# An attention and gated-MLP block in fp32 on one core: GpSimd's work pinned to program order, the fifth block's weights and the second pair's k strips loaded at other times, the last two heads' query blocks in another order, and loads of finished heads two ahead

## The chip, the core and the metric

The kernel runs on one core of one Trainium2 chip. The metric is the device time of one execution in microseconds (us); before the change it is 2733.96 us, the median of 3 runs (2732.69 to 2734.78). The engines are TensorE (PE, matmuls and transposes), VectorE (DVE), ScalarE (ACT), GpSimd (POOL) and SyncE (SP), each with its own instruction stream; SP issues most DMA transfers, POOL the rest.

## The reference

The input x is 2048 rows of D = 576. It is normalised, and goes through 32 heads of attention with 18 features each and through an MLP of width F = 4608 with a relu gate; the result is x plus attention times the silu of the MLP.

```python
xn = _layernorm(x, axis=-1)
s = _A_ref(xn, A_wqkv, A_wo)      # 32 heads, softmax(q k^T / sqrt(18)) v, then @ wo
g = _silu(_B_ref(xn, W_gate, W_up, W_down))   # h = relu(x W_gate) * (x W_up); h @ W_down
return x + s * g
```

## The kernel before

**Precision.** An fp32 product is made of three: each operand is split into a rounded part (hi) and the rest (lo), and hi x hi, hi x lo and lo x hi are added up (`PRODUCTS`, L97). Weights are split on POOL (`split_pool`, L93 to L95: a cast and a subtraction), results in PSUM on ACT and DVE (`split_full`, L89 to L91).

**Stage 1, up to 225 us.** Row groups of 512 (g = 0 to 3) are normalised, transposed and multiplied by the q, k and v weights. A group has four blocks of q and k columns (b = 0 to 3, `qk_block`), a fifth of 64 columns for two groups at once (`qk_last`, weights wqk4), and v (`v_block`). The results go from tiles of a ring of four ("hh": hh for q and k, ev for v) to DRAM (qd, kd, vd) by transfers that POOL issues (L300, L332). `weights` (L194) loads raw weights into a ring of two (rgw) by SP and splits them on POOL; `spill` (L282) writes a group's transposed rows to DRAM by SP.

**Stage 2, 225 to 2563 us.** 144 units, k = 36 x g + n. A unit takes 128 of the 4608 columns for one row group: `up(k)` multiplies by the gate and up weights (PE tile pg, weights gw, loaded and split one unit ahead by `up_weights(k + 1)`, ring of two), `up_end` makes h and its split hh (ACT hi, POOL lo, L461), and after every second unit `down` multiplies two units by the down weights dw into py and adds to y. Between the matmuls of a unit stand steps of attention of a pair of heads u = 0 to 15: `max_steps` (pm: row maxima of the scores of pair u + 1) and `exp_steps` (psx: scores of pair u, exponential p on ACT), then `attend` (po: p times va, the values with a column of ones). The first nine units hold only `max_steps` of pair 0, nine units go with each later pair. In units k < 9 ACT copies py and POOL adds it. `max_rows` (L543) writes the maxima of two query blocks (512 queries each) as extra rows into their qT tiles, by eight transfers of 2 KB on SP (L560), so that psx gives scores less the maximum. `load_q` and `load_k` load q and k strips from DRAM. `gate_steps` (L501) makes the silu of finished rows: exp on ACT, +1 and six reciprocals on DVE, a product on POOL, and a store to gd.

**Stage 3, 2563 us to the end.** Only the scores of the last pair (u = 15) are left, block by block (`exp_steps` with last=True), and between them runs the generator `outputs`: down(143), then for each tile k of 128 rows `heads(k)` (load 512 finished features o4 from od, transpose, split into hf), `rows_of` (gate row gt, input row xr), the product with wo (pw: `first4`, plus `last1` for the last 64 features, which come from o5 by `o5_rows`), gate, add, store. Tiles of query block 3 come first with their first 512 features alone, and are finished last.

**Order.** Instructions given to `tc.keep_in_program_order` keep their place behind the one traced before on their engine; for the others a scheduler chooses the order on their engine. PE's matmuls and transposes are all kept. PSUM has a ring of five banks for pm, psx and small transposes (`shared`), one for po, and a ring of two for pg, py, tps and pw (`bank`).

Of the kernel before, what the change touches and what calls it, by code (L numbers as in the profile page):

```python
# [19 lines left out]
def kernel(  # L20
# [68 lines left out]
    def split_full(dhi, dlo, ps):  # L89
        nc.scalar.activation(dhi, ps, AF.Copy)  # L90
        nc.vector.tensor_tensor(dlo, ps, dhi.bitcast(F32), ALU.subtract)  # L91

    def split_pool(hi, lo, raw):  # L93
        nc.gpsimd.tensor_copy(hi, raw)  # L94
        nc.gpsimd.tensor_tensor(lo, raw, hi.bitcast(F32), ALU.subtract)  # L95

# [65 lines left out]
    def max_steps(u, h):  # L162

        rows = slice(h * R, h * R + KA)
        for g in range(NQ):
            if h == 0:
                load_q(*((u, g + 1) if g + 1 < NQ else (u + 1, 0)))
                if g % 2 == 0:
                    mxs[u, g // 2] = at.tile([P, 2, 2, 4, NQ], F32, name="mx", bufs=2)
            mx = mxs[u, g // 2]  # L170
            qT = qTs[u, g]
            if h == 0 and g == 2:
                raw = two.tile([P, NT, HW], F32, name="raw", bufs=1)
                nc.sync.dma_start(raw, vd[u])
                va = vas[u % 2]
                for i in range(2):
                    nc.gpsimd.tensor_copy(va[:, :, i * VA : i * VA + DH], raw[:, :, i * DH : (i + 1) * DH])
            for j in range(4):
                js = slice(j * P, (j + 1) * P)
                for c in range(NQ):  # L180
                    ps = shared("pm")
                    mm(ps, qT[rows, js], kchunk(u, c)[rows, :], start=True, stop=True)
                    nc.vector.tensor_reduce(mx[:, g % 2, h, j, c : c + 1], ps, axis=AX.X, op=ALU.max)  # L183
                    if h and g % 2 and j == 3 and c == NQ - 1:
                        tasks.append((max_rows, ([qTs[u, g - 1], qT], mx)))
                    yield


    with ExitStack() as st:
# [30 lines left out]
        def stats(xt, ln):  # L220

            keep = tc.keep_in_program_order
            stat = one.tile([P, 4, 2, 6], F32, name="stat")
# [119 lines left out]
        def qk_weights(b):  # L343
# [11 lines left out]
            "wv", HC, [[[(wqkv, 2 * D + m * VH, VH)], [(wqkv, 2 * D + HC + m * VH, VH)]] for m in range(3)]  # L355
        )
        for _ in transposed(0, *ln0):
            pass
        for g in range(NQ):
# [12 lines left out]
            for b in range(4):  # L372
                qk_block(b, wqk[b], g, fill)
                if b == 0 and g == NQ - 1:
                    load_q(0, 0)
                    for c in range(NQ):
                        load_k(0, c)
                if b == 0 and g + 2 < NQ:
                    nxt = load_rows(g + 2)
                if b == 1 and g + 1 < NQ:  # L380
                    spill(g)
                if b == 2 and g == 0:
                    wqk.append(
                        weights("wqk4", P, [[[(wqkv, C4, DT), (wqkv, D + C4, DT)]] * 2], pl=ws, tag="gw")
                    )
            if fill is not None:
# [64 lines left out]
    def up_end(k, ps):  # L451
# [8 lines left out]
        nc.scalar.activation(hh[:, 0], h, AF.Copy)  # L460
        nc.gpsimd.tensor_tensor(hh[:, 1], h, hh[:, 0].bitcast(F32), ALU.subtract)  # L461
        hhs[k] = hh
# [3 lines left out]
    def down(k):  # L466
# [5 lines left out]
        for j in range(4):  # L472
            js = slice(j * P, (j + 1) * P)
            for n in range(2):
# [9 lines left out]
                if f == 1:  # L484
                    nc.scalar.activation(ys[j][:, cs], ps, AF.Copy)
                elif k < N1:
                    yt = pp.tile([P, 2, 2, 512], F32, name="p")[:, 0, 0, :HC]
                    nc.scalar.activation(yt, ps, AF.Copy)  # L488
                    nc.gpsimd.tensor_tensor(ys[j][:, cs], yt, ys[j][:, cs], ALU.add)
                else:  # L490
                    nc.vector.tensor_tensor(ys[j][:, cs], ps, ys[j][:, cs], ALU.add)  # L491
# [9 lines left out]
    def gate_steps():  # L501

        while gates:
# [5 lines left out]
            for n in range(6):  # L509
                yield  # L510
                cs = slice(n * GP, (n + 1) * GP)
                tc.keep_in_program_order(nc.vector.reciprocal(e[:, cs], e[:, cs]))
            nc.gpsimd.tensor_tensor(y, y, e, ALU.mult)
            nc.gpsimd.dma_start(gd[t * P : (t + 1) * P, :], y)
# [101 lines left out]
    ready = []  # L616
    pts = {}

    def exp_steps(u, h, ppool, done, last=False):
# [5 lines left out]
        if last:  # L625
            order = [(qc, qc, kt, kt // 2, kt % 2) for qc in range(NQ) for kt in range(NT)]
        else:
# [34 lines left out]
    def to_dram(u):  # L662
        ob = two.tile([P, NT, HW], F32, name="ob", bufs=1)

        def store(qp):
            if qp == NQ // 2 - 1:
                nc.sync.dma_start(od[:, u * HW : (u + 1) * HW].rearrange("(t p) d -> p t d", p=P), ob)

# [39 lines left out]
    up_weights(0)  # L708
    for c in range(NQ):
        load_k(1, c)  # L710
    k = 0
    for n in (4,) + (5, 7) * 4:
        emit_unit(k, None, 0, mx, n)
        k += 1
# [31 lines left out]
    o5 = f1.tile([P, NT, P], F32, name="o5")  # L746
    for d in range(2):
        nc.sync.dma_start(
            o5[:, :, d * DT : d * DT + U15], od[:, C4 : C4 + U15].rearrange("(t p) d -> p t d", p=P)
        )  # L750
    closed = []

    def done15(qc, po_):
# [5 lines left out]

    def heads(k):  # L760
        o4 = hp.tile([P, 512], F32, tag="h", name="o4")
        nc.sync.dma_start(o4, od[k * P : (k + 1) * P, 0:C4])
        ps = bank("tps")
        for c in range(4):
            tp(ps[:, c * P : (c + 1) * P], o4[:, c * P : (c + 1) * P], ident)
        hh = hp.tile([P, 2, 512], F32R, tag="hh", name="hf", bufs=4)
        split_full(hh[:, 0], hh[:, 1], ps)
        hq[k] = hh

    def rows_of(k):  # L770
# [21 lines left out]
    def o5_rows(qc):  # L792
        ps = bank("tps")
        for j in range(4):
# [8 lines left out]
    def outputs():  # L803
        for n, c in enumerate(down(len(units) - 1)):
            yield c if n % 2 else 2.0
        tail = [*range(3 * NQ, NT)]
        order = [*tail, *range(3 * NQ)]
        heads(order[0])
        gate_out()
        parts, g4 = {}, {}  # L810

        def next_heads(k):
            i = order.index(k) + 1
            if i < NT:
                heads(order[i])
                return 0.45
            return 0.0

        for k in tail:
# [10 lines left out]
            gate_out()  # L830
        for qc in range(NQ - 1):
            while qc not in closed:
# [3 lines left out]
            for j in range(4):  # L836
# [9 lines left out]
                nc.gpsimd.tensor_tensor(xt, xt, gt, ALU.add)  # L846
                nc.sync.dma_start(out2[k * P : (k + 1) * P, :], xt)
        gts = [rows_of(k)[0] if k < tail[3] else None for k in tail[:3]]
        while NQ - 1 not in closed:
            yield 10.0  # L850
        o5T = o5_rows(NQ - 1)
        yield 0.45
        for j, k in enumerate(tail):
            gt = gts[j] if j < 3 else rows_of(k)[0]
            t = parts[k]
            for cs in halves:
                ps = bank("pw")[:, :HC]
                project(ps, last1(o5T, j, cs))
                nc.vector.tensor_tensor(gt[:, cs], ps, gt[:, cs], ALU.mult)
                (nc.vector if j == 3 else nc.gpsimd).tensor_tensor(t[:, cs], t[:, cs], gt[:, cs], ALU.add)  # L860
                yield 2 * 0.133
            nc.sync.dma_start(out2[k * P : (k + 1) * P, :], t)

    outs = outputs()
    due = 0.0
    for n, _ in enumerate(zip(*[exp_steps(NU - 1, h, pp, done15, True) for h in range(2)])):
        if n % 2:
            if len(ready) > 1:
                attend()
            run_tasks()  # L870
            due = min(due, 1.0) + 2.2
# [38 lines left out]
```

## Time and profile before

| | us |
|---|---|
| median of 3 runs | 2733.96 |
| profiled execution, its own time | 2735.94 |
| its span | 2734.1 |
| PE busy | 2677.4 |
| DVE busy | 1909.5 |
| ACT busy | 1476.7 |
| POOL busy | 1202.1 |
| first unit starts | 225.09 |
| first scores of the last stage | 2564.66 |

Times in rows count from the span's start. A row of the order in time has start, duration, engine, line, operation, output<-input, count, and in brackets how long the engine stood idle before it and whom it waited for. A row of a waits view has waiter, releaser, total, number of times, longest. A row of a windows view has the stretch, its length, the busy time and count of PE, PEld (weight loads), DVE, ACT and POOL, then PE's granted clock (1.00 is full), the share of DMA and GB/s.

### The profile page before, as it was taken

The numbers are of one execution on the slowest core, as the hardware profiler recorded it, in microseconds if no ns is written. First come the engines' busy times: TensorE is split into PE (matmuls) and PEld (weight loads), VectorE is DVE, ScalarE is ACT, GpSimd is POOL, SyncE is SP. The second block draws the span as 40 slices with busy tenths as digits, with TensorE's granted clock in tenths as the row PEclk, the third lists the DMA queues.
The fourth block names the chain that finished last, engine by engine and source line by source line (L and its number), as shares of the span: only waits on it lengthen the run. The fifth ranks groups of instructions, "written<-read, shape, count | busy, mean of one in ns | idle before, by whom it ended". The sixth has DMA issues, their size and how long they took to land.

```text
span 2734.1 us, 55210 instructions
## 1 busy us (share of the span) xinstructions
PE 2677.4 (98%) x22100; PEld 2014.3 (74%) x22100; DVE 1909.5 (70%) x3248; ACT 1476.7 (54%) x2686; POOL 1202.1 (44%) x931
## 2 busy tenths in 40 slices
PE   8998999999999999999999999999999999999988
PEld 6787877777777777777777777777777777777655
DVE  5326777777777877777777877777777777777542
ACT  3321256565656555565666555555556565655554
POOL 4235844444444444444444544444444444444322
PEclk9999999999999999999999999999999999999999
DMA  9745322223262322223352323232432323221344
GB/s 252 191 154 147 75 62 70 71 71 79 67 144 74 80 69 77 68 70 69 82 137 72 82 67 75 72 78 63 119 85 70 78 70 76 66 72 48 82 133 146
DMA packets 290128, 250.17 MB, mean 91 GB/s; under 512 B 60048, under 2 KB 231824, under 8 KB 289872
## 3 DMA queue, kind: packets, MB, share of 16 engines
q1 hardware_dynamic: 281808, 218.32, 31.9%
q0 software_dynamic: 8064, 28.32, 3.1%
q8 instruction: 175, 2.87, 0.4%
q14 instruction: 81, 0.66, 0.1%
HBM read 201.51 MB, written 44.53 MB: 90 GB/s over the span
## 4 chain that ended last, share of the span: by engine, by line
PE 91%; DMA 3%; POOL 2%; ACT 1%; SPq 1%; DVE 1%; issue 1%; DVEq 0%; POOLq 0%; ACTq 0%
PE pg L64 29%; PE py L64 17%; PE po L64 16%; PE pm L64 12%; PE psx L64 10%; PE pq L64 3%; PE pw L64 2%; PE pv L64 1%; PE tps L67 1%; PE tp L67 1%; DMA rgw<-in_A_wqkv_dram 0%; POOL gw L95 0%; ACT p L637 0%; DMA rd<-in_B_W_down_dram 0%; DMA qd<-hh 0%
## 5 line engine op out<-in xcount | busy, mean ns | idle before, releaser
L183 DVE TENSOR_REDUCE mx<-pm 128x1 f32<-128x512 f32 x2048 | 1360.5, 687 | 288.5 <-PE pm L64 179.4
L637 ACT ACTIVATE p<-psx 128x512 f32<-128x512 f32 x2048 | 1169.0, 598 | 573.7 <-PE psx L64 477.8
L64 PE MATMUL pg<-x,gw 64*128 64x512 f32 x7668 | 1367.2, 394 | 9.9 <-POOL gw L94 6.5
L64 PEld LDWEIGHTS pg<-x,gw 64*128 64x128 f32 x7668 | 1051.4, 186 | 125.7 <-POOL gw L94 7.0
L64 PE MATMUL psx<-qT,kT 56*128 56x512 f32 x2048 | 780.1, 398 | 0.4 <-ACT p L637 0.4
L64 PE MATMUL pm<-kT,qT 54*128 54x512 f32 x2048 | 776.9, 405 | 0.7 <-ACT p L488 0.6
L64 PEld LDWEIGHTS py<-dw,hh 128*128 128x128 f32 x3456 | 460.5, 188 | 63.3 <-issue 57.8
L64 PE MATMUL py<-dw,hh 128*128 128x288 f32 x3456 | 478.9, 297 | 1.4 <-POOL hh L461 0.8
L64 PE MATMUL po<-p,va 128*32 128x512 f32 x4096 | 474.7, 597 | 0.0
L64 PEld LDWEIGHTS pm<-kT,qT 54*128 54x128 f32 x2048 | 359.0, 185 | 120.6 <-issue 61.1
L491 DVE TENSOR_TENSOR y<-py,y 128x288 f32<-128x288 f32 x520 | 237.8, 458 | 295.1 <-PE py L64 295.1
L64 PEld LDWEIGHTS psx<-qT,kT 56*128 56x128 f32 x2048 | 366.6, 186 | 43.1 <-issue 5.0
L94 POOL CAST gw<-rg 128x1152 fp32r<-128x1152 f32 x144 | 165.0, 1146 | 516.5 <-PE pg L64 280.8
L94 POOL CAST dw<-rd 128x576 fp32r<-128x576 f32 x144 | 95.9, 666 | 673.5 <-PE py L64 295.5
L95 POOL TENSOR_TENSOR gw<-rg,gw 128x1152 fp32r<-128x1152 f32 x144 | 383.2, 2661 | 11.6
L64 PEld LDWEIGHTS po<-p,va 128*32 128x32 f32 x4096 | 115.9, 109 | 262.7 <-issue 256.2
L95 POOL TENSOR_TENSOR dw<-rd,dw 128x576 fp32r<-128x576 f32 x144 | 206.2, 1432 | 11.2
L461 POOL TENSOR_TENSOR hh<-h,hh 128x512 fp32r<-128x512 f32 x144 | 186.3, 1294 | 10.9 <-ACT hh L460 10.9
L460 ACT ACTIVATE hh<-h 128x512 fp32r<-128x512 f32 x144 | 90.8, 631 | 169.4 <-DVE h L458 169.4
L64 PE MATMUL pq<-x,wqk 64*128 64x512 f32 x972 | 123.1, 401 | 3.7 <-ACT ev L327 3.7
L456 ACT ACTIVATE r<-pg 128x512 f32<-128x512 f32 x144 | 85.8, 596 | 62.1 <-PE pg L64 34.2
L64 PEld LDWEIGHTS pq<-x,wqk 64*128 64x128 f32 x972 | 98.4, 186 | 19.9 <-issue 4.2
(88 smaller groups left out, 1110.3 us busy)
## 6 DMA issues: line engine op xcount, KB each, us to landing
rg<-in_B_W_gate_dram SPq DMA_DIRECT2D x144, 288.0 KB
rg<-in_B_W_up_dram SPq DMA_DIRECT2D x144, 288.0 KB
rd<-in_B_W_down_dram SPq DMA_DIRECT2D x144, 288.0 KB
x<-xTd SPq DMA_DIRECT2D x54, 256.0 KB
qT<-qd SPq DMA_DIRECT2D x384, 36.0 KB
kT<-kd SPq DMA_DIRECT2D x384, 36.0 KB
qd<-hh POOLq DMA_DIRECT2D x16, 512.0 KB, 3.7
kd<-hh POOLq DMA_DIRECT2D x16, 512.0 KB, 4.8
```

Source lines behind the costliest of these rows:

```text
L64: return tc.keep_in_program_order(nc.tensor.matmul(*args, **kw))
L67: return tc.keep_in_program_order(nc.tensor.transpose(*args))
L94: nc.gpsimd.tensor_copy(hi, raw)
L95: nc.gpsimd.tensor_tensor(lo, raw, hi.bitcast(F32), ALU.subtract)
L183: nc.vector.tensor_reduce(mx[:, g % 2, h, j, c : c + 1], ps, axis=AX.X, op=ALU.max)
L456: nc.scalar.activation(r, ps[0], AF.Relu)
L460: nc.scalar.activation(hh[:, 0], h, AF.Copy)
L461: nc.gpsimd.tensor_tensor(hh[:, 1], h, hh[:, 0].bitcast(F32), ALU.subtract)
L491: nc.vector.tensor_tensor(ys[j][:, cs], ps, ys[j][:, cs], ALU.add)
L637: nc.scalar.activation(pts[key][:, h, i, :], ps, AF.Exp, scale=SCALE)
```

## The change

1. On POOL the splits of weights (`split_pool`), the copies va<-raw, the lo part of hh, the additions of y and the gate product are kept in program order. The copies va<-raw are written one group of queries later (g = 3).
2. wqk4, the fifth block's weights, is loaded right behind wv and not after block 2.
3. The k strips of pair 1 are written in units 2 to 5 and not ahead of unit 0.
4. In the last pair the query blocks go in the order 3, 0, 2, 1; the tiles that are finished last are those of block 1.
5. A pair's results are stored to od in two halves.
6. `heads` loads two tiles ahead; the transposes of `heads` and `o5_rows` take a bank of the ring of five. The transposes of po's results run ahead of the next `attend`, and the o5T of the last block is made two tiles earlier. One more of the final additions is on DVE.

```diff
+    def keep(ins):
+        return tc.keep_in_program_order(ins)
+
     def split_pool(hi, lo, raw):
-        nc.gpsimd.tensor_copy(hi, raw)
-        nc.gpsimd.tensor_tensor(lo, raw, hi.bitcast(F32), ALU.subtract)
+        keep(nc.gpsimd.tensor_copy(hi, raw))
+        keep(nc.gpsimd.tensor_tensor(lo, raw, hi.bitcast(F32), ALU.subtract))
...
             if h == 0 and g == 2:
                 raw = two.tile([P, NT, HW], F32, name="raw", bufs=1)
-                nc.sync.dma_start(raw, vd[u])
+                keep(nc.sync.dma_start(raw, vd[u]))
+            if h == 0 and g == 3:
                 va = vas[u % 2]
                 for i in range(2):
-                    nc.gpsimd.tensor_copy(va[:, :, i * VA : i * VA + DH], raw[:, :, i * DH : (i + 1) * DH])
+                    keep(
+                        nc.gpsimd.tensor_copy(va[:, :, i * VA : i * VA + DH], raw[:, :, i * DH : (i + 1) * DH])
+                    )
...
+        wqk.append(weights("wqk4", P, [[[(wqkv, C4, DT), (wqkv, D + C4, DT)]] * 2], pl=ws, tag="gw"))
         for _ in transposed(0, *ln0):
...
-                if b == 2 and g == 0:
-                    wqk.append(
-                        weights("wqk4", P, [[[(wqkv, C4, DT), (wqkv, D + C4, DT)]] * 2], pl=ws, tag="gw")
-                    )
...
-        nc.gpsimd.tensor_tensor(hh[:, 1], h, hh[:, 0].bitcast(F32), ALU.subtract)
+        keep(nc.gpsimd.tensor_tensor(hh[:, 1], h, hh[:, 0].bitcast(F32), ALU.subtract))
...
-                    nc.gpsimd.tensor_tensor(ys[j][:, cs], yt, ys[j][:, cs], ALU.add)
+                    keep(nc.gpsimd.tensor_tensor(ys[j][:, cs], yt, ys[j][:, cs], ALU.add))
...
-            nc.gpsimd.tensor_tensor(y, y, e, ALU.mult)
+            keep(nc.gpsimd.tensor_tensor(y, y, e, ALU.mult))
...
+    LASTQ = (3, 0, 2, 1)
...
-            order = [(qc, qc, kt, kt // 2, kt % 2) for qc in range(NQ) for kt in range(NT)]
+            order = [(qc, qc, kt, kt // 2, kt % 2) for qc in LASTQ for kt in range(NT)]
...
-            if qp == NQ // 2 - 1:
-                nc.sync.dma_start(od[:, u * HW : (u + 1) * HW].rearrange("(t p) d -> p t d", p=P), ob)
+            ts = slice(qp * NT // 2, (qp + 1) * NT // 2)
+            nc.sync.dma_start(od[:, u * HW : (u + 1) * HW].rearrange("(t p) d -> p t d", p=P)[:, ts], ob[:, ts])
...
-    for c in range(NQ):
-        load_k(1, c)
     k = 0
     for n in (4,) + (5, 7) * 4:
+        if 2 <= k < 2 + NQ:
+            load_k(1, k - 2)
         emit_unit(k, None, 0, mx, n)
...
-    for d in range(2):
-        nc.sync.dma_start(
-            o5[:, :, d * DT : d * DT + U15], od[:, C4 : C4 + U15].rearrange("(t p) d -> p t d", p=P)
-        )
...
+    tail = [*range(4 * LASTQ[3], 4 * LASTQ[3] + 4)]
+    horder = [*tail, *(4 * qc + j for qc in LASTQ[:3] for j in range(4))]
...
+    o4s = {}
+
+    def load_heads(k):
+        o4s[k] = hp.tile([P, 512], F32, tag="h", name="o4")
+        nc.sync.dma_start(o4s[k], od[k * P : (k + 1) * P, 0:C4])
+
+    def heads(i):
+        k = horder[i]
+        o4 = o4s.pop(k)
+        ps = shared("tps")
         for c in range(4):
             tp(ps[:, c * P : (c + 1) * P], o4[:, c * P : (c + 1) * P], ident)
         hh = hp.tile([P, 2, 512], F32R, tag="hh", name="hf", bufs=4)
         split_full(hh[:, 0], hh[:, 1], ps)
         hq[k] = hh
+        if i + 2 < NT:
+            load_heads(horder[i + 2])
...
-        ps = bank("tps")
+        ps = shared("tps")
...
-        tail = [*range(3 * NQ, NT)]
-        order = [*tail, *range(3 * NQ)]
-        heads(order[0])
+        heads(0)
+        yield 0.45
+        heads(1)
         gate_out()
-        parts, g4 = {}, {}
+        parts = {}
 
         def next_heads(k):
-            i = order.index(k) + 1
+            i = horder.index(k) + 2
             if i < NT:
-                heads(order[i])
+                heads(i)
                 return 0.45
             return 0.0
...
-        for qc in range(NQ - 1):
+        end, since = None, 0
+        for qc in LASTQ[:3]:
             while qc not in closed:
                 yield 10.0
...
+                if LASTQ[3] in closed and end is None:
+                    since += 1
+                    if since == 2:
+                        end = o5_rows(LASTQ[3])
         gts = [rows_of(k)[0] if k < tail[3] else None for k in tail[:3]]
-        while NQ - 1 not in closed:
+        while LASTQ[3] not in closed:
             yield 10.0
-        o5T = o5_rows(NQ - 1)
+        o5T = end if end is not None else o5_rows(LASTQ[3])
...
-                (nc.vector if j == 3 else nc.gpsimd).tensor_tensor(t[:, cs], t[:, cs], gt[:, cs], ALU.add)
+                (nc.vector if j > 1 else nc.gpsimd).tensor_tensor(t[:, cs], t[:, cs], gt[:, cs], ALU.add)
...
+    for k in horder[:2]:
+        load_heads(k)
+    for d in range(2):
+        nc.sync.dma_start(
+            o5[:, :, d * DT : d * DT + U15], od[:, C4 : C4 + U15].rearrange("(t p) d -> p t d", p=P)
+        )
     outs = outputs()
     due = 0.0
     for n, _ in enumerate(zip(*[exp_steps(NU - 1, h, pp, done15, True) for h in range(2)])):
         if n % 2:
+            run_tasks()
             if len(ready) > 1:
                 attend()
-            run_tasks()
```

Three places where the order moves. **POOL in the first row group** (qd, kd: stores of q and k, a pair for each block b; wv, wqk: splits). Before:

```order
L300 DMA qd<-hh 128x2x512 [waits DVE_49]
L95 TENSOR_TENSOR wv<-rgw,wv 128x9x96 [waits Pool_49]
L300 DMA kd<-hh 128x2x512 [waits DVE_49]
L300 DMA qd<-hh 128x2x512 [waits DVE_49]
L300 DMA kd<-hh 128x2x512 [waits DVE_49]
L94 CAST wqk_576<-rgw 128x1152 [waits DMAHW6_49,DMAHW7_49,DMAHW5_49,DMAHW0_49]
L95 TENSOR_TENSOR wqk_576<-rgw,wqk_576 128x1152 [waits Pool_49]
```

and with the change:

```order
L305 DMA qd<-hh 128x2x512 [waits DVE_49]
L98 TENSOR_TENSOR wv<-rgw,wv 128x9x96 [waits Pool_49]
L305 DMA kd<-hh 128x2x512 [waits DVE_49]
L97 CAST wqk_172<-rgw 128x1152 [waits DMAHW6_49,DMAHW7_49,DMAHW5_49,DMAHW0_49]
L98 TENSOR_TENSOR wqk_172<-rgw,wqk_172 128x1152 [waits Pool_49]
L305 DMA qd<-hh 128x2x512 [waits DVE_49]
L305 DMA kd<-hh 128x2x512 [waits DVE_49]
```

The split of wqk4 has moved ahead of the stores of block 2.

**POOL around units 0 to 2** (va: cleared by MEMSET; gw: a unit's weights; dw: down weights; raw: v loaded back). Before:

```order
L534 MEMSET va_2954 128x832
L94 CAST dw<-rd 128x576
L535 MEMSET va_2954 128x16
L536 MEMSET va_2954 128x16
L95 TENSOR_TENSOR dw<-rd,dw 128x576
L177 COPY va_2950<-raw 128x16x18 x2
L94 CAST dw<-rd 128x576
L95 TENSOR_TENSOR dw<-rd,dw 128x576
L177 COPY va_2954<-raw 128x16x18 x2
L94 CAST gw<-rg 128x1152
L95 TENSOR_TENSOR gw<-rg,gw 128x1152
L461 TENSOR_TENSOR hh<-h,hh 128x512
```

and with the change:

```order
L538 MEMSET va_2954 128x16
L97 CAST gw<-rg 128x1152
L98 TENSOR_TENSOR gw<-rg,gw 128x1152
L97 CAST gw<-rg 128x1152
L98 TENSOR_TENSOR gw<-rg,gw 128x1152
L463 TENSOR_TENSOR hh<-h,hh 128x512
L97 CAST gw<-rg 128x1152
L98 TENSOR_TENSOR gw<-rg,gw 128x1152
L97 CAST dw<-rd 128x576
L98 TENSOR_TENSOR dw<-rd,dw 128x576
```

The splits for units 0 and 1, which stood among the stores of stage 1, now follow the clearing of va; the one for unit 2 has come ahead of the dw splits, and the copies of raw have left this stretch.

**PE and SP at the start of stage 3** (psx: scores; qT_33484: the q tile of block 3; nt: the maxima that `max_rows` has just made for blocks 2 and 3; o4: loads of finished heads). PE before and then with the change:

```order
L67 MATMUL tp2_34518<-ident_69,ot_34461 128x128 x3
L64 MATMUL psx_34532<-qT_31957,kT6_2324 128x512 [waits DMAHW6_49,DMAHW5_49]
L64 MATMUL psx_34535<-qT_31957,kT6_2324 128x512 [waits DMAHW7_49,DMAHW0_49]
L64 MATMUL psx_34538<-qT_31957,kT6_2324 128x512
L64 MATMUL psx_34541<-qT_31957,kT6_2324 128x512 [waits Activation_49]
```
```order
L67 MATMUL tp2_34533<-ident_69,ot_34476 128x128 x3
L64 MATMUL psx_34551<-qT_33484,kT6_2324 128x512 [waits DMAHW6_49,DMAHW5_49]
L64 MATMUL psx_34554<-qT_33484,kT6_2324 128x512 [waits DMAHW7_49,DMAHW0_49]
L64 MATMUL psx_34557<-qT_33484,kT6_2324 128x512
L64 MATMUL psx_34560<-qT_33484,kT6_2324 128x512 [waits Activation_49]
L64 MATMUL py_34563<-dw_34295,hh_34210 128x288 [waits DVE_49,PE_49,Pool_49]
```

SP with the change:

```order
L739 DMA rw_34499<-in_A_wo_dram 128x576 [waits DMAHW6_49,DMAHW0_49,Pool_49]
L562 DMA qT_33037<-nt_34523 1x4x128 [waits Activation_49]
L562 DMA qT_33037<-nt_34523 1x4x128
L562 DMA qT_33037<-nt_34523 1x4x128 [waits DMAHW1_49]
L742 DMA rw_34504<-in_A_wo_dram 64x576 [waits DMAHW5_49,DMAHW2_49,Pool_49]
L742 DMA rw_34504<-in_A_wo_dram 64x576 [waits DMAHW3_49]
L562 DMA qT_33037<-nt_34523 1x4x128 [waits DMAHW4_49]
L562 DMA qT_33484<-nt_34523 1x4x128
L562 DMA qT_33484<-nt_34523 1x4x128 [waits DMAHW6_49]
L562 DMA qT_33484<-nt_34523 1x4x128 [waits DMAHW7_49]
L562 DMA qT_33484<-nt_34523 1x4x128 [waits DMAHW0_49]
L670 DMA od_79<-ob_32568 128x8x36 [waits DMAHW1_49,DVE_49]
```

The first scores of the last pair read block 0's tile (qT_31957) before, and block 3's with the change. The four transfers into it are the last of the eight, as before, and py of the last `down` still follows the scores.

More of the change, by code (lines that the diff above doesn't have):

```diff
@@ L220, in stats @@
         def stats(xt, ln):
-            keep = tc.keep_in_program_order
             stat = one.tile([P, 4, 2, 6], F32, name="stat")
@@ L758 @@
     hq = {}
-    def heads(k):
-        o4 = hp.tile([P, 512], F32, tag="h", name="o4")
-        nc.sync.dma_start(o4, od[k * P : (k + 1) * P, 0:C4])
-        ps = bank("tps")
+    o4s = {}
[6 more added lines that the diff above has]
+        ps = shared("tps")
         for c in range(4):
@@ L792, in o5_rows @@
     def o5_rows(qc):
-        ps = bank("tps")
+        ps = shared("tps")
         for j in range(4):
```

## The prediction

> **What bounds the kernel now.** I read the page's busy times, then TensorE's waits, then windows over the long middle, and last the order of time around each wait.
>
> ```profile
> PE 2677.4 (98%) x22100; PEld 2014.3 (74%) x22100; DVE 1909.5 (70%) x3248; ACT 1476.7 (54%) x2686; POOL 1202.1 (44%) x931
> ...
> PE 91%; DMA 3%; POOL 2%; ACT 1%; SPq 1%; DVE 1%; issue 1%; DVEq 0%; POOLq 0%; ACTq 0%
> ```
> ```profile
> PE pg L64 <- POOL gw L94: 6.5, 1, 6.5
> PE tp L67 <- ACT ot L567: 5.8, 5, 1.5
> PE pw L64 <- DVE hf L91: 5.0, 4, 2.0
> PE tps L67 <- DMA o<-od: 5.0, 1, 5.0
> PE pw L64 <- DVE o5T L798: 3.8, 3, 1.4
> PE pq L64 <- ACT ev L327: 3.7, 1, 3.7
> ```
> ```profile
> 700.00:1000.00 300.00, 300.00 (x2452) 223.16 (x2450) 228.72 (x387) 176.60 (x317) 138.02 (x102) 1.00 0.36 90
> ```
> TensorE (PE) is busy 98% of the span and makes 91% of the chain that ended last. The window shows the middle: 300.00 of 300 us busy at full clock, GpSimd (POOL) 138. The edit removes no matmul there, so nothing is to be won. What can move are the waits in the second list (us in total, times, longest): 3.7 us near 72 us, 6.5 near 247 us, and 19.6 after 2563 us.
>
> A wait also costs clock. In the next rows the column before the last two is the granted clock of PE:
>
> ```profile
> 72.00:76.00 4.00, 4.00 (x22) 3.22 (x24) 0.00 (x0) 1.01 (x3) 0.88 (x2) 0.57 1.01 241
> 250.00:254.00 4.00, 3.92 (x20) 3.15 (x22) 1.60 (x3) 0.00 (x0) 3.92 (x4) 0.56 0.59 143
> 2586.70:2596.00 9.30, 8.68 (x37) 5.86 (x38) 5.78 (x10) 4.16 (x8) 1.58 (x2) 0.55 0.30 90
> ```
> They lie just behind three of the waits, and PE was busy nearly throughout. Lost to the clock: 4 x 0.43 = 1.7 us behind the first, 4 x 0.44 = 1.7 behind the second, and behind the third 9.3 x 0.45 = 4.2, less 0.3 for a short wait inside it, 3.9.
>
> **Part 1: the fifth block's weights (b=4) load earlier.**
>
> ```profile
> 34.79 2.06 POOL L95 TENSOR_TENSOR wv<-rgw,wv 128x864 fp32r<-128x864 f32 x1
> 45.57 7.59 SPq L130 DMA_DIRECT2D rgw<-in_A_wqkv_dram  x4
> 46.77 0.73 POOL L300 DMA_DIRECT2D qd<-hh  x1 [3.93 <-DVE hh L91]
> 57.88 1.14 POOL L94 CAST wqk<-rgw 128x1152 fp32r<-128x1152 f32 x1 [9.67 <-DMA rgw<-in_A_wqkv_dram]
> 61.73 0.73 POOL L300 DMA_DIRECT2D qd<-hh  x1
> 71.51 0.41 ACT L327 ACTIVATE ev<-pv 128x288 f32<-128x288 f32 x1 [9.85 <-DMA qd<-hh]
> 71.97 12.31 PE L64 MATMUL pq<-x,wqk 64*128 64x512 f32 x90 [3.68 <-ACT ev L327]
> ```
> GpSimd waits 9.67 us for these weights, splits them, and only then issues block 3's stores at 61.73. ScalarE's ev waits for a buffer that those stores read, and PE waits 3.68 us for ev. In the change the split stands ahead of block 2's stores, and its four loads are issued behind wv's, ahead of the spills, instead of at 45.57. The loads took 57.88 - 53.16 = 4.7 us after the last of their issues (45.57 + 7.59). Now they need only the buffer that wv's second split frees at 36.85: issued from 37 to 44.5 they land by 49, and the split ends near 53. Block 2's stores, ready at 46.77, go out some 6 us later; block 3's go 6 us earlier than 61.73, and ev comes in time. At stake are 3.68 + 1.7 = 5.4 us. Lower bound 0, if block 2's later stores hold a buffer instead. I take **4.8**, since two blocks lie between those stores and ev.
>
> **Part 2: GpSimd in program order, units 0 to 2.** The early splits of units 0 and 1 (gw, at 188 and 206 us) now stand behind the clearing of va.
>
> ```profile
> 206.47 1.14 POOL L94 CAST gw<-rg 128x1152 fp32r<-128x1152 f32 x1 [3.14 <-PE pq L64]
> 207.70 2.67 POOL L95 TENSOR_TENSOR gw<-rg,gw 128x1152 fp32r<-128x1152 f32 x1
> 225.08 0.79 POOL L534 MEMSET va<- 128x832 f32 x1 [7.06 <-PE pv L64]
> 227.66 0.81 POOL L534 MEMSET va<- 128x832 f32 x1
> ```
> ```profile
> 225.09 1.64 PE L64 MATMUL pg<-x,gw 64*128 64x512 f32 x10
> 233.19 0.50 PE L64 MATMUL pg<-x,gw 64*128 64x512 f32 x1 [0.43 <-ACT r L456]
> 247.38 1.22 PE L64 MATMUL pg<-x,gw 64*128 64x512 f32 x4 [6.51 <-POOL gw L94]
> 250.08 0.79 PE L64 MATMUL pg<-x,gw 64*128 64x512 f32 x2 [1.48 <-POOL gw L95]
> 259.27 2.92 PE L64 MATMUL py<-dw,hh 128*128 128x288 f32 x20
> ```
> A split takes 3.9 us (206.47 to 210.37). The clearing waits for the last pv at 225.08 and ends near 228.6, so unit 0's low halves are ready at 232.5, and PE, ready at 225.09, has only a few matmuls before. From there unit 0 takes its 8.1 us (to 233.19), less 0.7 already done, plus 1.7 of clock: 241.6. Unit 1 (233.19 to 247.38 - 6.51, 7.7 us) ends at 249.3. The old wait of unit 2, 6.51 + 1.48, came from dw splits and va copies ahead of its gw split. Now that split stands right behind unit 0's hh: buffer free at 241.6, hh near 244.8, split done at 248.7, so no wait. Unit 2 (9.2 us, less 1.7 of clock, plus 0.6 for the matmuls done early) ends at 257.4 instead of 259.27. I take a gain of **1.7**, bounds -1 (3.9 us of clock) and +3. In the rest of the middle the pinned splits have 300 - 138 us of slack and the k strips still land among the q strips: 0.
>
> **Part 3: the tail.** What goes: `heads` loads come two ahead and no longer wait for the whole store (5.0 and 3.9 of clock); hf 5.0; transposes of ot run ahead of the next scores, three waits of 1.47, 4.4; o5T, two of 1.18, 2.4.
>
> ```profile
> 2607.46 0.66 PE L67 MATMUL tp<-ident,ot 128*128 128x128 f32 x4 [1.47 <-ACT ot L567]
> 2660.01 1.85 PE L64 MATMUL pw<-wo,hf 128*128 128x288 f32 x12 [1.18 <-DVE o5T L798]
> ```
> That is **20.7**. What comes: query block 3 is now first, and its maxima are the last ones computed.
>
> ```profile
> 2564.66 0.73 PE L64 MATMUL psx<-qT,kT 56*128 56x512 f32 x4
> 2568.13 1.84 SPq L560 DMA_DIRECT2D qT<-nt  x3
> 2572.24 3.19 SPq L560 DMA_DIRECT2D qT<-nt  x5
> 2576.12 0.66 POOL L94 CAST wo<-rw 128x576 fp32r<-128x576 f32 x1 [3.35 <-DMA rw<-in_A_wo_dram]
> gd<-y POOLq DMA_DIRECT2D x16, 288.0 KB, 2.4
> ```
> Before, the first scores ran at 2564.66, on block 0. The last of eight small transfers of maxima was issued by 2575.43, and in the changed order nothing on SyncE (SP) makes this earlier: they still stand behind the same wo loads, which wait for splits. PE now needs the last four, and down(143) stands behind the scores. Landing: at least 0; at most 4.2 us, as the wo load before them (issues end at 2571.88, used at 2576.12); I take 2.4, the gate store's row and the nearest short one. So PE stands 2575.43 + 2.4 - 2564.66 = **13.2** (10.8 to 15.0), plus clock of **2.0** (1.7 to 3.9), nearer to the first two waits, since scores and not transposes follow.
>
> The Trainium skill ("DMA: Bandwidth & Descriptors", Anatomy of one DMA — SWDGE (gpsimd) path) gives some 2.0 us of fixed cost to a transfer of GpSimd's kind; by it the wait would be an estimated 12.8 and the time 0.4 lower.
>
> A second new wait: the third head's load goes into a buffer that the first head's transposes free, and its transposes stand right behind the second's.
>
> ```profile
> 2583.00 3.64 DMA o<-od
> 2596.99 0.60 PE L67 MATMUL tps<-ident,o 128*128 128x128 f32 x4
> 2725.76 2.96 DMA gt<-gd
> ```
> Loads take 3.64 or, at the end, 2.96; 0.60 of transposes covers part: 2.4 to 3.0, I take **2.7**, and no clock, since every drop seen followed at least 3.68 us.
>
> The Trainium skill ("TensorE: Matmul & The Clock Gate", Part 4: PE-mode transpose) says that transposes do not count as busy for the clock as matmuls do. The trace fits: 3.9 us were lost where eight transposes followed the wait, 1.7 where matmuls did. By that rule this wait with its transposes also drops the clock, and the estimate is about 2 us more, 2726.7.
>
> Tail: 20.7 - 13.2 - 2.0 - 2.7 = **2.8**, bounds 20.7 - 10.8 - 1.7 - 2.4 = 5.8 and 20.7 - 15.0 - 3.9 - 3.0 = -1.2. Store halves and DVE's extra add lie beside PE work; uncovered, an add is 0.45 us.
>
> **Sum.** 4.8 + 1.7 + 2.8 = 9.3 us. The profiled execution took 2735.94 (span 2734.1, 1.8 around it), 2.0 above the median of the runs. The sum taken from the median gives 2733.96 - 9.3 = **2724.7**; from the profiled one, 2726.6.
>
> **Rivals.**
> *Slower: the shared banks.* Twenty transposes of heads and o5 move from the two banks of "gen" into the ring of five in which scores wait.
>
> ```profile
> 2590.19 3.80 DVE L512 RECIPROCAL e<-e 128x96 f32<-128x96 f32 x6
> ```
> A bank is held until VectorE has subtracted, behind up to 3.80 us of reciprocals, while scores come back to it after about one group of four. If each of the twenty costs 1.0 us, a wait as hf's (5.0 in four), the time is 2744.7; it is slower from (9.3 + 5.5) / 20 = 0.74 us each. Against it: only four such bursts fall in the tail, and ACT is 54% busy.
> *No change: ev still waits,* now for block 2's stores: 2724.7 + 4.8 = 2729.5. For it speaks that these really go out 6 us later.
> *It does not do what it says in the tail:* hf, ot and o5T wait for ScalarE and VectorE, not for loads, so 5.0 + 4.4 + 2.4 = 11.8 us stay: 2736.5. For it: the releasers named are DVE and ACT; against: the split now has a whole head's projection as cover, two groups like the one at 2660.01 (1.85 us).
> *More gain:* the maxima go out ahead of the wo loads and the wait is 4 us with no more than 1.7 of clock: 2724.7 - 9.2 - 0.3 = 2715.2. The order of the change speaks against it.
>
> **How the numbers follow.** Forecast 0.62, shared banks 0.12, ev 0.11, tail waits stay 0.11, more gain 0.04. A measurement can tell 0.2%, 5.5 us: faster is below 2728.5, slower above 2739.4. The forecast's own range, with ends of single terms, is 2719 to 2731, some 0.06 of its chance above 2728.5. Faster 0.56 + 0.04 = 0.60; within 0.2% 0.06 + 0.22 = 0.28; slower 0.12. The range for 8 in 10 reaches up over both cases near no change and down over part of the larger gain: 2716 to 2737.
>
> **What would show it.** Part 1: ev's wait at 72 us gone from PE's list. Part 2: a wait of 4 to 7 us at 225 us, none at 247. Part 3: psx waiting for qT some 13 us from about 2558 with half clock after; hf, o5T and o<-od almost gone; a wait of 2 to 3 us at the third head. The prediction is wrong if psx waits for score banks in the tail, if PE shows waits between 400 and 2550 us, or if the first scores of the tail do not wait.

## The result, and the profile after

| | before | changed |
|---|---|---|
| median of 20 runs, us | 2731.89 | 2732.01 |
| range, us | 2729.16 to 2735.93 | 2728.53 to 2737.54 |
| profiled execution, us | 2735.94 | 2731.45 |
| its span, us | 2734.1 | 2729.7 |

The ratio of the changed kernel to the one before is 1.0, with a 95% interval of 0.9993 to 1.0007; in a second session it was 0.9994 (0.9985 to 1.0002). The change does nothing that these measurements can tell. The two traces differ by 4.5 us and the runs by 0.1, because the profiled execution of before is the slowest of its 20. So what a trace gains has to be tried in runs.

The first view after is the list of TensorE's waits in the changed kernel (total, times, longest, in us).

```profile
PE tps L67 <- ACT xn L260: 12.0, 2, 11.3
PE psx L64 <- DMA qT<-nt: 10.5, 2, 10.2
PE pg L64 <- POOL gw L97: 4.2, 1, 4.2
PE psx L64 <- DVE mx L189: 2.9, 3, 1.0
PE tps L67 <- DMA o<-od: 2.3, 1, 2.3
PE pg L64 <- ACT r L458: 2.2, 5, 0.6
PE pg L64 <- POOL gw L98: 1.5, 1, 1.5
PE pw L64 <- DVE o5T L807: 1.4, 1, 1.4
```

The wait for ev is gone, and so is hf; psx now waits for the maxima, unit 0 for gw, the third head for its load. All that was forecast. The row that was not is the fourth, three waits for score banks. It is short, but the distance between the same instruction in both traces shows that it is the one that matters. Here is ScalarE's r at the end of units 2, 36, 39, 40, 76, 112 and 143, from the order in time, of before and then of the changed kernel:

```profile
258.99 0.60 ACT L456 ACTIVATE r<-pg 128x512 f32<-128x512 f32 x1 [16.01 <-PE pg L64]
787.50 0.59 ACT L456 ACTIVATE r<-pg 128x512 f32<-128x512 f32 x1
839.13 0.60 ACT L456 ACTIVATE r<-pg 128x512 f32<-128x512 f32 x1
851.86 0.60 ACT L456 ACTIVATE r<-pg 128x512 f32<-128x512 f32 x1 [0.17 <-PE pg L64]
1446.99 0.60 ACT L456 ACTIVATE r<-pg 128x512 f32<-128x512 f32 x1 [0.17 <-PE pg L64]
2042.13 0.60 ACT L456 ACTIVATE r<-pg 128x512 f32<-128x512 f32 x1
2559.52 0.60 ACT L456 ACTIVATE r<-pg 128x512 f32<-128x512 f32 x1
```
```profile
252.44 0.60 ACT L458 ACTIVATE r<-pg 128x512 f32<-128x512 f32 x1 [6.20 <-PE pg L64]
780.48 0.59 ACT L458 ACTIVATE r<-pg 128x512 f32<-128x512 f32 x1
831.94 0.60 ACT L458 ACTIVATE r<-pg 128x512 f32<-128x512 f32 x1
846.66 0.60 ACT L458 ACTIVATE r<-pg 128x512 f32<-128x512 f32 x1 [0.17 <-PE pg L64]
1443.69 0.60 ACT L458 ACTIVATE r<-pg 128x512 f32<-128x512 f32 x1 [0.17 <-PE pg L64]
2041.01 0.60 ACT L458 ACTIVATE r<-pg 128x512 f32<-128x512 f32 x1 [0.17 <-PE pg L64]
2558.41 0.60 ACT L458 ACTIVATE r<-pg 128x512 f32<-128x512 f32 x1
```

The changed kernel is ahead by 6.55, 7.02, 7.19, then 5.20, 3.30, 1.12 and 1.11 us. It loses nearly 2 us in unit 40, 76 and 112 each, four units into every later row group, and nowhere else in the middle. From unit 39 to 112 that is 6.07 us, and 5.74 in a second trace of the same kernel. Between units 39 and 40 VectorE and GpSimd do this in the changed kernel (start, duration):

```profile
837.47 2.34 DVE L510 TENSOR_SCALAR e<-e 128x576 f32<-128x576 f32 x1
839.74 1.87 DVE L189 TENSOR_REDUCE mx<-pm 128x1 f32<-128x512 f32 x3
```
```profile
834.35 1.29 POOL L463 TENSOR_TENSOR hh<-h,hh 128x512 fp32r<-128x512 f32 x1 [3.07 <-ACT hh L462]
835.59 1.15 POOL L97 CAST gw<-rg 128x1152 fp32r<-128x1152 f32 x1
836.82 2.68 POOL L98 TENSOR_TENSOR gw<-rg,gw 128x1152 fp32r<-128x1152 f32 x1
```

and in the one before:

```profile
844.52 0.45 DVE L508 TENSOR_SCALAR e<-e 128x576 f32<-128x576 f32 x1
```
```profile
838.59 1.14 POOL L94 CAST gw<-rg 128x1152 fp32r<-128x1152 f32 x1
839.82 2.66 POOL L95 TENSOR_TENSOR gw<-rg,gw 128x1152 fp32r<-128x1152 f32 x1
842.46 1.29 POOL L461 TENSOR_TENSOR hh<-h,hh 128x512 fp32r<-128x512 f32 x1
```

Before, gw was split at once and hh followed; GpSimd was idle when VectorE added 1 to e, which took 0.45 us. Now gw is pinned behind hh, GpSimd first stands idle for 3.07 us, and the split runs under e + 1, which takes 2.34 us and ends 0.3 us behind the split. The reductions of maxima behind it come late, their banks come free late, and PE waits:

```profile
840.47 0.50 PE L64 MATMUL psx<-qT,kT 56*128 56x512 f32 x1 [0.96 <-DVE mx L189]
```

The idle time named is 0.96 us. The rest of the 1.99 lost in this unit stands in the record as busy time: from the one r to the next, at full clock, the same 109 matmuls count 13.76 us busy, and 12.73 before.

### The profile page after: what moved, and what is told of

Its sections match the earlier page's. It is cut to its first block, busy times and chain, and to the rows that moved or that the text cites. A ratio compares the mean times of both kernels' runs of the same rounds, so it can differ in the third digit from the quotient of the medians.

```text
span 2729.7 us, 55255 instructions
## 1 busy us (share of the span) xinstructions
PE 2681.5 (98%) x22100; PEld 2013.2 (74%) x22100; DVE 1916.1 (70%) x3250; ACT 1475.1 (54%) x2686; POOL 1200.6 (44%) x929
## 4 chain that ended last, share of the span: by engine, by line
PE 94%; POOL 2%; ACT 1%; issue 1%; DVE 1%; DMA 1%; SPq 0%; DVEq 0%; POOLq 0%; ACTq 0%
PE pg L64 29%; PE py L64 17%; PE po L64 17%; PE pm L64 12%; PE psx L64 10%; PE pq L64 4%; PE pw L64 2%; PE pv L64 2%; PE tps L67 1%; PE tp L67 1%; POOL gw L98 0%; POOL y L491 0%; POOL dw L98 0%; ACT p L640 0%; DVE e L510 0%
## 5 line engine op out<-in xcount | busy, mean ns | idle before, releaser
L556 ACT ACTIVATE nt<-tp 32x128 fp32r<-32x128 f32 x32 | 8.5, 266 | 193.3 <-PE tp L67 193.3
```

The lines of the kernel that those rows point to most:

```text
L556: nc.scalar.activation(nt_.bitcast(F32R), ps[0:32, 0:P], AF.Copy)
```

## The experiments

The theory was: the pins put GpSimd's split under VectorE's e + 1 and cost some 5.5 us in three places, the first scores' wait for the maxima costs 13 us, and the gains of the other parts are real but eaten by these two. The wait for the maxima had been forecast, and with it the last stage was still to gain 2.8 us; the first of the two had not. Medians of before differ from session to session (2731.9 to 2736.5), so ratios to before in the same session are used; 0.1% is 2.7 us. The intervals reach some 2.5 us to either side, so a difference between two of the ratios is uncertain by an estimated 3.5 us. The traces tell the loss in the middle more closely: it is the change of the distance to before from unit 39 to 112.

**e + 1 on ScalarE.**

```diff
-tc.keep_in_program_order(nc.vector.tensor_scalar(e, e, 1.0, None, op0=ALU.add))
+tc.keep_in_program_order(nc.scalar.activation(e, e, AF.Copy, bias=1.0))
```

> The changed kernel, with e + 1 of the silu (16 times) done on ScalarE and not on VectorE. Theory P: in the changed order GpSimd's split of a unit's weights runs at the moment of VectorE's e + 1 and holds it up (2.34 us for 0.45, three times, once in each later row group), PE loses some 1.9 us each time. Then the three steps of the distance to before (near units 40, 76 and 112) are gone, and the time is 5.5 to 6 us under the changed kernel's 2732.0, about 2726. Rival: VectorE is simply full there, and the wait for score banks comes from the order of its other work; then the steps stay and the time is 2731 to 2733.

Ratio 0.9977 (0.9966 to 0.9987), against 0.9994 for the changed kernel some 4.6 us less. The waits for score banks are gone from the list. Of the three steps 0.4, 0.2 and 0.1 us remain. From unit 39 to 112 its trace loses 1.16 us where the changed kernel's loses 6.07. The theory holds. The 1.16 us are not a hold: the kernel before with the same move (x7, below) loses 1.16 us over the same units, and that is why the gain is somewhat under the forecast.

**e + 1 on VectorE in another form.** It stays in its place and also writes the sum of its output.

```diff
-nc.vector.tensor_scalar(e, e, 1.0, None, op0=ALU.add)
+nc.vector.tensor_scalar(e, e, 1.0, 0.0, op0=ALU.add, op1=ALU.add, accum_out=es)
```

> The changed kernel with e + 1 on VectorE in the same place, but as the form of the instruction that also sums its output. Theory: what holds e + 1 up is a way into SBUF that the plain form takes together with GpSimd's split and this form does not; then all 16 take the same time, some 0.6 to 0.8 us, the steps at units 40, 76 and 112 go and the time is 4 to 5 us under the changed kernel's. Rival: VectorE is held up by GpSimd's split whatever the form; then three of them still take 2.3 us or more.

The view of this line has count, then minimum, median and maximum in ns; first the changed kernel's, then this one's:

```profile
L510 DVE TENSOR_SCALAR e<-e x16: 449/452/2339, 796.0 to 2619.3; 128x576 f32<-128x576 f32 x16
```
```profile
L511 DVE TENSOR_SCALAR_CACHE_REDUCE e<-e x16: 741/744/753, 797.0 to 2615.3; 128x576 f32<-128x576 f32 x16
```
```profile
838.58 0.74 DVE L511 TENSOR_SCALAR_CACHE_REDUCE e<-e 128x576 f32<-128x576 f32 x1
```
```profile
836.69 1.13 POOL L97 CAST gw<-rg 128x1152 fp32r<-128x1152 f32 x1
837.91 2.69 POOL L98 TENSOR_TENSOR gw<-rg,gw 128x1152 fp32r<-128x1152 f32 x1
```

It runs in the middle of GpSimd's split, slower than the plain form alone, and is not held up. Ratio 0.9983 (0.9974 to 0.9991), some 3 us under the changed kernel, where 4 to 5 were expected; that difference alone is not clear of the noise. In its trace 2.06 us are lost from unit 39 to 112 for 6.07, and no wait for score banks is left in the middle. So it is the form of the instruction, and not GpSimd's presence as such, that decides. The Trainium skill says it in these terms ("SBUF — State Buffer", Who interferes with whom): VectorE and GpSimd share one pair of ports that is held for a whole instruction; `tensor_scalar` may take it, the form with an accumulator does not. These runs agree: 2.34 us against 0.74.

**gw not pinned.**

```diff
-split_pool(gw[:, 0], gw[:, 1], rg)
+split_pool(gw[:, 0], gw[:, 1], rg, False)   # False: no keep() on its two instructions
```

> The changed kernel with no split of gate and up weights (gw) pinned, all else as it is, e + 1 on VectorE. Theory: it is the pin of gw that puts a unit's split behind the hh of the unit before and so under e + 1, and that puts units 0 and 1 behind the clearing of va. Then both go: the steps at units 40, 76, 112 are 0, unit 0 does not wait, and the time is 13 to 15 us under the changed kernel's. Rival: other pins (hh, dw) make the steps; then only unit 0's 9 us go.

Ratio 0.9968 (0.9958 to 0.9978), about 7 us under the changed kernel, half of what was expected. The steps in units 40, 76 and 112 are gone against before, and unit 0 does not wait. In the trace 0.53 us are lost from unit 39 to 112. But the scheduler put unit 1's hh behind the next split of gw, and the first `down` now waits for it; the distance falls by 7.61 us from unit 2 to unit 3. From the list of PE's waits:

```profile
PE py L64 <- POOL hh L464: 5.9, 3, 4.6
```

So it is gw's pin that makes the steps, and the pins of the other splits alone do not hold units 2 and 3 together.

**The pins alone on the kernel before.**

```diff
-        nc.gpsimd.tensor_copy(hi, raw)
-        nc.gpsimd.tensor_tensor(lo, raw, hi.bitcast(F32), ALU.subtract)
+        keep(nc.gpsimd.tensor_copy(hi, raw))
+        keep(nc.gpsimd.tensor_tensor(lo, raw, hi.bitcast(F32), ALU.subtract))
...
-        nc.gpsimd.tensor_tensor(hh[:, 1], h, hh[:, 0].bitcast(F32), ALU.subtract)
+        keep(nc.gpsimd.tensor_tensor(hh[:, 1], h, hh[:, 0].bitcast(F32), ALU.subtract))
...
```

> The kernel before with GpSimd's pins alone (splits, va copies one query group later, hh, y, gate product). Theory: unit 0 waits and unit 2 does not, some 1 us gained there, and e + 1 is held up in each later row group, 5.5 us lost: 3 to 5 us slower than before. Rival: the holds need the other parts of the change (they shift the phase between GpSimd and VectorE); then within 2 us of before.

Ratio 1.0011 (1.0002 to 1.0020), 3.0 us slower; e + 1 takes up to 2.34 us again, three times, and the steps in units 40, 76 and 112 are 1.9, 1.8 and 1.9 us. As expected: the pins do it without the other parts.

**e + 1 on ScalarE in the kernel before.**

```diff
-            tc.keep_in_program_order(nc.vector.tensor_scalar(e, e, 1.0, None, op0=ALU.add))
+            tc.keep_in_program_order(nc.scalar.activation(e, e, AF.Copy, bias=1.0))
```

> The kernel before with e + 1 on ScalarE alone. Theory: e + 1 was never held up there (0.45 to 0.46 us in all 16), so nothing is gained: within 2 us of before. Rival: ScalarE's version frees VectorE in general; then 3 us or more are gained here too.

0.9996 (0.9987 to 1.0005): nothing that the runs can tell, as expected. Where nothing is held, the move brings nothing.

**The first two splits of gw not pinned.**

```diff
-split_pool(gw[:, 0], gw[:, 1], rg)
+split_pool(gw[:, 0], gw[:, 1], rg, k > 1)
```

> The changed kernel, with the weight splits of units 0 and 1 not pinned, so that they stand among the stores of the first stage again; all others pinned. Theory: unit 0's wait (4.25 + 1.48 us) and its slow clock (about 4 us) go, and unit 2 does not wait either, since its split still stands ahead of the down weights; 8 to 10 us less, about 2723. Rival: the wait moves to unit 2 as it was before the change (6.5 us); then 2730 to 2733.

0.9955 (0.9943 to 0.9968), some 10.7 us under the changed kernel. In the trace r of unit 0 comes 8.94 us earlier and r of the last unit 9.05: the gain stays. Unit 2 does not wait.

**Block 0 first.**

```diff
-LASTQ = (3, 0, 2, 1)
+LASTQ = (0, 3, 2, 1)
```

> The changed kernel, with the query blocks of the last pair in the order 0, 3, 2, 1. Theory: the first scores of block 3 wait for maxima that land late (10.2 + 0.4 us, and some 3 us of slow clock behind it), all of it on the path; then about 13 us go, 2719. Rival: the wait hides other late work (the loads of wo and of finished heads), which then shows as a new wait of 5 us or more; then 2724 to 2728.

0.9947 (0.9935 to 0.9960), some 12.8 us under the changed kernel. The trace is 9.6 us shorter. The rival's new wait is there, though, and takes part of it: the third head's load is issued behind the transfers of o5, gt and xr.

```profile
2587.35 1.08 PE L67 MATMUL tps<-ident,o 128*128 128x128 f32 x4 [5.26 <-DMA o<-od]
```

**The fifth block's weights alone, on the kernel before.**

```diff
+        wqk.append(weights("wqk4", P, [[[(wqkv, C4, DT), (wqkv, D + C4, DT)]] * 2], pl=ws, tag="gw"))
...
-                if b == 2 and g == 0:
-                    wqk.append(
-                        weights("wqk4", P, [[[(wqkv, C4, DT), (wqkv, D + C4, DT)]] * 2], pl=ws, tag="gw")
-                    )
```

> The kernel before, with the earlier load of the fifth block's weights alone. Theory: the wait for ev near 72 us goes and the time falls by 4.8 us against before (2727). Rival: the wait of 3.7 us belongs to the profiled execution of before, 4 us above its median, and is mostly absent in others; then the time is within 2 us of before.

0.9989 (0.9980 to 0.9998), 3.0 us (0.5 to 5.5): between the two. The wait for ev is gone in its trace. What the first stage gained was lost again in two places: unit 2's wait for gw grew from 6.5 to 7.2 us, and one tiny VectorE instruction was held up under GpSimd, with PE waiting 3.98 us for the normalised rows behind it:

```profile
29.53 3.34 DVE L239 TENSOR_TENSOR ln<-ln,ln 128x4 f32<-128x4 f32 x1
```
```profile
29.99 2.02 POOL L95 TENSOR_TENSOR wv<-rgw,wv 128x864 fp32r<-128x864 f32 x1
31.94 0.91 POOL L94 CAST wv<-rgw 128x864 fp32r<-128x864 f32 x1
```

**The last stage alone, on the kernel before** (the changed kernel without pins, with the weights and strips as before).

```diff
-        wqk.append(weights("wqk4", P, [[[(wqkv, C4, DT), (wqkv, D + C4, DT)]] * 2], pl=ws, tag="gw"))
...
+    for c in range(NQ):
+        load_k(1, c)
...
-        if 2 <= k < 2 + NQ:
-            load_k(1, k - 2)
```

> The kernel before with the changes of the last stage alone (order 3, 0, 2, 1, loads two ahead, store in halves, shared banks). Theory, from the two traces: 2 to 3 us less than before. Rival: the tail gains nothing, since the wait for the maxima takes all that the loads give; then within 1 us, or slower.

0.9991 (0.9982 to 1.0000), 2.5 us (0 to 4.9), as the theory has it, though only just clear of nothing.

**No pins.** This is the changed kernel with every new pin taken off, and the copies va<-raw written where they were before.

```diff
-        keep(nc.gpsimd.tensor_copy(hi, raw))
-        keep(nc.gpsimd.tensor_tensor(lo, raw, hi.bitcast(F32), ALU.subtract))
+        nc.gpsimd.tensor_copy(hi, raw)
+        nc.gpsimd.tensor_tensor(lo, raw, hi.bitcast(F32), ALU.subtract)
...
```

> The changed kernel without any of GpSimd's pins: the earlier fifth block's weights, the k strips and the last stage are left. Theory: the gains of the first and the last stage stand without the loss in the middle, 2.6 to 4.8 and 2.5 us: 5 to 7 us under before. Rival: the pins are needed for the gain near 72 us; then 2 to 3 us.

0.9987 (0.9978 to 0.9996), 3.6 us less than before, under the theory's 5 to 7. No e + 1 in the middle takes more than 0.45 us, and from unit 39 to 112 the trace loses 0.54 us. Unit 0 starts as early as in the changed kernel, but unit 2 waits longer:

```profile
PE pg L64 <- POOL gw L97: 9.6, 1, 9.6
```

In this trace r is 6.10 us ahead of before in unit 0 and 1.98 in unit 2. The split of unit 2 stands behind two dw splits that wait for their loads. So in this trace the early weights pay in full only with the pins, which put that split first; the trace with these weights alone hands 1.17 us back there.

**The changed kernel again.**

> The changed kernel as it is, a second time, so that its time and trace stand beside the other runs. Theory: 0 within 2 us of before in time, and the same three waits as in its first trace: psx for nt 10 us, gw of unit 0 4.2 + 1.5, e + 1 held up three times (2.3 us each). Rival: the holds of e + 1 are an accident of one execution; then they are gone or stand elsewhere.

0.9994 (0.9985 to 1.0002), with the same three waits and the same three holds of 2.34 us. They belong to the kernel, not to one execution. One more e + 1, in the last stage, takes 1.91 us in both traces; it does so without pins too (1.92) and not with the pins alone (0.46), so it comes with the new order of that stage.

**All mended.** e + 1 on ScalarE, block 0 first, two free splits, and the loads of heads three ahead:

```diff
-o4s[k] = hp.tile([P, 512], F32, tag="h", name="o4")
+o4s[k] = f2.tile([P, 512], F32, name="o4")   # a ring of three
-if i + 2 < NT:
-    load_heads(horder[i + 2])
+if i + 3 < NT:
+    load_heads(horder[i + 3])
...
-for k in horder[:2]:
+for k in horder[:3]:
```

> The changed kernel with e + 1 on ScalarE, the order 0, 3, 2, 1, the first two gw splits free, and three loads of finished heads ahead from a ring of three. Theory, adding the parts by their traces (4.5 + 9.5 + 9 + 5): 28 us under the changed kernel, a ratio to before of about 0.990. Rival: the parts overlap (another wait takes the place of the third head's load), and the ratio is 0.993 or more.

2703.34 us, ratio 0.9888 (0.9875 to 0.9900), 30.6 us faster than before and some 29 under the changed kernel, where 28 were expected. The parts add up. All waits of PE over 2 us in its trace:

```profile
PE tps L67 <- ACT xn L261: 11.9, 2, 11.1
PE pw L64 <- DVE gt L874: 2.5, 3, 1.9
PE pg L64 <- ACT r L459: 2.4, 5, 0.6
```

## Why the prediction was right or wrong

The forecast was 2724.7 us, faster by 9.3; measured is no change. Its range holds the result, its likeliest case does not. That the result lies in the range is luck in part: the range reached up to 2737 for rivals of which none came about. The prediction also named signs of being wrong. One was PE waiting between 400 and 2550 us, and PE does so three times, 0.96 us each, for score banks; in the trace of before it never does.

*"In the rest of the middle the pinned splits have 300 - 138 us of slack ...: 0."* This is the step that failed. The slack is there, and no matmul waits for a split of weights after unit 0. But the step asked only whether GpSimd would be late, not what its split, moved in time, runs beside. The cost is some 6 us in the trace (7.19 - 1.12 = 6.1 from unit 39 to 112), and e + 1 on ScalarE gives 4.6 of it back in runs. Among the rivals was none with this mechanism, though the trace of before had both durations, 0.45 for e + 1 and 3.9 for a split.

*Part 1, 4.8 us.* The mechanism was right: no trace with the early weights has the wait for ev. Its size came from one execution, and the slowest. The wait's length in profiled executions that load these weights late:

```profile
PE pq L64 <- ACT ev L327: 3.7, 1, 3.7
```
```profile
PE pq L64 <- ACT ev L329: 5.2, 1, 5.2
```
```profile
PE pq L64 <- ACT ev L332: 1.9, 1, 1.9
```

These are before, the last stage alone and the pins alone; before with e + 1 on ScalarE has none, and r of its unit 0 comes 5.80 us ahead of before's without the early weights. So most of the lead with which the changed kernel's trace enters the middle may be the slow execution of before. The part measured alone 3.0 us. It also leaned on part 2 more than the text saw: without the pins, in that one trace, unit 2 hands two thirds of it back.

*Part 2, 1.7 us.* Unit 0 waits as forecast (4.25 and 1.48 us), unit 2 not at all. The distance at unit 2, 6.55, is 0.55 more than the 6.00 at the clearing of va (225.08 before, 219.08 after); by unit 36 it is 7.02. Right mechanism, a third to 0.6 of the size. The term that was short is the clock behind unit 0's wait, taken as 1.7 us:

```profile
224.00:232.00 8.00, 6.52 (x30) 4.62 (x32) 1.38 (x2) 0.00 (x0) 6.20 (x3) 0.50 0.62 170
```

PE is busy 6.52 us there at half clock, which loses 3.3 us.

*Part 3, 2.8 us.* The sum was right, 2.5 us in runs, but by luck: its terms were off both ways and their errors cancel. These are the first scores and the third head in the changed kernel, SP's last issues of maxima, and PE's windows behind both waits:

```profile
2573.78 0.76 PE L64 MATMUL psx<-qT,kT 56*128 56x512 f32 x1 [10.16 <-DMA qT<-nt]
2574.93 1.22 PE L64 MATMUL psx<-qT,kT 56*128 56x512 f32 x3 [0.39 <-DMA qT<-nt]
...
2597.01 0.67 PE L67 MATMUL tps<-ident,o 128*128 128x128 f32 x4 [2.34 <-DMA o<-od]
2597.39 3.17 PE L64 MATMUL pw<-wo,hf 128*128 128x288 f32 x12
```
```profile
2570.68 3.16 SPq L562 DMA_DIRECT2D qT<-nt  x5
```
```profile
2576.00:2582.00 6.00, 6.00 (x29) 4.17 (x29) 0.92 (x2) 3.25 (x7) 0.00 (x0) 0.63 1.01 202
2597.00:2604.00 7.00, 6.99 (x40) 5.53 (x41) 4.45 (x8) 3.23 (x6) 2.01 (x2) 0.76 0.20 66
```

The wait for the maxima is 10.55 us where 13.2 was taken and 10.8 was the lower bound. The last issue ends at 2573.84 and the scores that need it start at 2574.93, a landing of 1.1 us where the gate store's 2.4 was taken: that row was of 288 KB, these are 2 KB. The estimate of 12.8 us for the wait, given beside it, was too long as well. The rest of the difference is the issues, which end 10.2 us after PE is ready (2573.84 - 2563.62) where 10.8 was taken, and the first matmul, which ran for 0.76 us ahead of the last landing. Clock behind it: 6 x 0.37 = 2.2 and some 0.9 ahead of 2576, 3.1 in place of 2.0. The third head waits 2.34 us for 2.7, but it does cost clock, 7 x 0.24 = 1.7 us. "No clock, since every drop seen followed at least 3.68 us" was wrong. The Trainium skill's rule, weighed there, that transposes do not count as busy ("TensorE: Matmul & The Clock Gate", Part 4: PE-mode transpose), came nearer: the wait stood between twelve transposes, and its estimate was about 2 us. What was to go from the tail went: hf, the three waits of ot, two of o5T. With the measured terms the sum is 20.7 - 10.55 - 3.1 - 2.3 - 1.7 = 3.0 us. From r of the last unit to the end the traces gain 3.4 us in both executions of the changed kernel and 2.0 in both without pins.

*Rivals.* The shared banks cost nothing that PE's list shows but one wait of psx in the tail, 0.46 us; the prediction had named such a wait as a sign too, but at this size it decides nothing. The wait for ev did not come back, and the tail's waits did not stay. The time that the second and the third rival gave, no change, came about by another mechanism.

*The frame.* The profiled execution was taken as 2.0 us above the median; with 20 runs it is 4.0 above. A sum of waits from such a trace promises more than a typical run can give back. Put together as an estimate, part 1 by its runs, part 2 and the middle by the traces and part 3 by its runs: 3.0 + 0.8 - 6.0 + 2.5 = 0.3 us, which is the change that does nothing.

## What to carry to other kernels

An order that is moved on GpSimd is to be held against VectorE's instructions that fall under it, not only against those that wait for GpSimd. A loss spread over a long stage is found by the distance between the same instruction in two traces, not by the list of waits, where it was 2.9 of some 6 us. Of the parts of a stage, the one whose inputs were sent last should not run first: that one number in the order was worth 10 to 13 us.

## What had not been expected of the hardware

A VectorE instruction on 128x4 elements, 0.16 us in the trace of before, took 3.34 us under two GpSimd instructions, in the execution with the early weights alone. Such holds come and go from trace to trace: the same instruction takes 0.88 us in the changed kernel's first trace and 0.16 in its second, 0.89 us in the kernel before with e + 1 on ScalarE. Together with the wait for ev, which was 0 to 5.2 us in executions with the same order of that stage, they may be why runs of one kernel spread over 6 to 11 us; that was not tried.
